# Eight more rows of the second batch's first stage in the prologue, and reads and writes on other queues: a fused spectral filter and feed-forward kernel

## The chip, the cores and the metric

The kernel runs on one core of one Trainium2 chip. The metric is the device time of one execution in microseconds; lower is better. A core has a matrix engine (PE, with its weight loads shown apart as PEld), a vector engine (DVE), an activation engine (ACT), a general engine (POOL) and a sequencer for transfers (SP). SP, ACT and POOL can all issue DMA transfers; those of one issuing engine are issued in the order of the program. Every engine works through its own list of instructions in order and waits on semaphores where it needs another's result.

## The reference

All arrays are float32 except the two weight matrices, which come as float64 (8-byte words) and are turned into float32 on the chip.

```python
X = np.fft.rfft(x, axis=1)                       # x: (8, 3008, 256)
Y = X * (filt_r + 1j * filt_i)[None, :, :]
y = np.fft.irfft(Y, n=3008, axis=1).astype(np.float32)
h = y.reshape(24064, 256) @ w_in                 # (256, 2048)
g = h - np.tanh(h)
out = (g @ w_out).astype(np.float32)             # (2048, 256)
```

## The kernel before

**The transforms.** The sequence of 3008 is split as 64 x 47 (`NQ`, `NR`). The *first stage* is, for each of the 47 residues r, a transform over the 64 positions; residues r and 47 - r are taken together as one "row" of 128 partitions, so a batch has 24 rows (`NH`). One row is one matmul: 128 x 128 matrix, 128 x 256 data. Results go to a scratch tensor in device memory, `ct1[b]`. The *second stage* goes across the rows, multiplies with the filter and goes back; its results are in `ct2[b]`. The *last stage* reads 4 rows of `ct2[b]` (tile `e2`) and makes `ut`, up to 512 tokens in transposed form: these are one *group*; a batch has 6 groups (`NC`), the kernel 48. `last(i, z)` does it: matmuls into two PSUM banks `pu` (even and odd), a copy of the odd one by ACT, an add and a subtract by DVE into `ut`.

**The feed-forward part.** Each group goes through four units (u = 0 to 3, a quarter of the 2048 hidden columns each; unit number U = 4i + u): the product with `w_in` (`up_plain` for U below 4, `up` behind), the nonlinearity on ACT and DVE (`shrink`), the product with `w_out` (`down_plain`, `down`). `up` and `down` use a seven-product scheme with prepared sums of weights, `up_plain` and `down_plain` the plain products. The weights lie in `wu` and `wd`, `[128, 7, 1024]` each: parts 0, 1, 3 and 6 hold the converted weights, parts 2, 4 and 5 (and 6, later) the sums, which `sums` writes from the first group on.

**The prologue** (up to the first unit) runs batch 0 through its first and second stage with everything kept on chip where possible. The second stage of batch 0 runs over seven slots of frequencies (loop over `g`, 0 to `last_g` = 6): `across` (transposes), `forth` (over the rows), `filtered`, and `back0` or, for the last slot, `back`. The ways back are put off by one slot (`ended`, `way_back`). Each writes its part of `ct2[0]`; `rest(a, n, queues)` reads slots a to a + n of it into `e2` with four transfers, one for each of four blocks, dealt over the queues given. Beside that the prologue converts the first five weight parts (`convert`, from the generator `early`; the order of its instructions among the others is the order in which the code calls it).

**Batch 1 and 2.** In the prologue `first1(x1)` does rows 0 to 7 of batch 1's first stage: `x1` is loaded by `load_x` on SP at g == 2; four PSUM banks of two rows each are copied by ACT into `two` (a half of the kept tile `xy`, then the tile `a1`) and written to `ct1[1]` with four transfers on SP. The other rows of batch 1 (c = 2 to 5, four rows each) and all of batch 2 are done by the generator `first(2, z2, also)`: each step (`next(firsts[2])`) is four matmuls, two ACT copies and one write issued by ACT, and starts the loads of the step after next on SP. In the main loop the places of these steps are set by the list `due`, in positions 20c + 5u + k (k = 0 to 4, five places in each unit): in group 0 a step may stand at any place that is due, later only at u < 3 and k == 2. `NX` is 6, `LEAD` 34.

**The tail of the prologue**, in program order: `rest` for slots 0 to 4 on SP, the last way back (its copies at L481, its writes at L483 on ACT and SP in turn), `rest` for the last two slots on SP, the start of `first` (two loads), the rest of the conversions, `first1(x1)`, the start of the later conversions, and eight matmuls that feed nothing (`warmer`). Then `last(0, z2)`, four more such matmuls (L1374) and the first unit. The tile tags `e1` (two or four buffers), `big` (three buffers) and `xy` (two halves in turn, `buffer("xy")`) are shared: `x1` and the later conversions use buffers that others have left.

Of the kernel before, what the change touches and what calls it, by code (L numbers as in the profile page):

```python
# [117 lines left out]
def kernel(  # L118
# [144 lines left out]
    def load_x(t, b, r, n):  # L263

        nc.sync.dma_start(t[0:64, 0:n, :], dram(x.tensor, (b * SEQ + r) * DM,
                                                [[NR * DM, 64], [1, n * DM]]))
        lo = 1 if r == 0 else 0
        if lo:
            nc.sync.dma_start(t[64:128, 0, :], dram(x.tensor, b * SEQ * DM,
                                                    [[NR * DM, 64], [1, DM]]))  # L270
        nc.sync.dma_start(t[64:128, lo:n, :], dram(x.tensor, (b * SEQ + NR - r - lo) * DM,
                                                   [[NR * DM, 64], [-DM, n - lo], [1, DM]]))
        return t
# [310 lines left out]
    def last(i, z, held=False):  # L584
# [13 lines left out]
        even, odd = banks  # L598
        for k in (1, 0) if held else (1,):
# [3 lines left out]
        u4 = ut.rearrange("p h (j n) -> p h j n", n=128)  # L603
        m = sum(w == 128 for w in widths(c))
# [3 lines left out]
        if i == 0:  # L608
            uts[i] = (ut, None, w)
            yield  # L610
            return
# [420 lines left out]
    with tc.tile_pool(name="tr", bufs=2) as tr, tc.manual_schedule():  # L1032
# [16 lines left out]
        with tc.tile_pool(name="pro", bufs=1) as pro, \  # L1049
# [172 lines left out]
            def first1(x1):  # L1222

                for r in range(0, 8, 2):
                    pf = z0("pf", [128, 2, DM])
                    for k in range(2):
                        nc.tensor.matmul(pf[:, k], f0[:, r + k], x1[:, r + k],
                                         start=True, stop=True)
# [4 lines left out]
                    ACT.copy(a1, pf)  # L1233
                    nc.sync.dma_start(
                        dram(ct1[1], r * DM, [[NH * DM, 128], [1, 2 * DM]]), a1)
                    yield
# [286 lines left out]
```

## Time and profile before

| | us |
|---|---|
| median of 3 runs | 2541.87 |
| lowest, highest | 2540.63, 2543.5 |
| profiled execution | 2542.18 |
| its span in the trace | 2540.3 |

| engine | busy us | share of the span |
|---|---|---|
| PE | 2522.6 | 99% |
| DVE | 1935.6 | 76% |
| ACT | 1694.2 | 67% |
| POOL | 1532.0 | 60% |

The trace is of one execution. Its span leaves out what lies around the program; the profiled execution's own time is 1.9 us longer than its span. Names in the trace are those of the program with the numbers left out: `x1` shows as `x`, `ct1` and `ct2` as `ct`, `a1` and `a2` as `a`. L and a number is the line of the kernel. In a timeline row the columns are start, length, engine, line, operation, output and inputs, shapes, number of instructions merged, and in brackets the idle time of the engine ahead of it with what ended it. A matmul of float32 shows as two records. The ends of matmuls are modelled, so lengths of consecutive PE rows overlap by a little; times from start to start are exact.

### The profile page before, as it was taken

To read this page: it belongs to the slowest core of one execution; us is meant where nothing else is said; L and a number is where in the kernel's file an instruction comes from. 1 tells how busy PE (TensorE), PEld (TensorE's weight loads), DVE (VectorE), ACT (ScalarE), POOL (GpSimd) and SP (SyncE) were. 2 spreads that over 40 slices of the span, in tenths; PEclk is the share of its full clock that TensorE was granted. 3 is DMA by queue.
4 is the path that set the end of the run, shared out by engine and by line. 5 is a ranking of instruction groups with operands and counts; after the bars stand their busy time and mean duration, and the time that the engine had idled before them with its cause. 6 is when DMAs were issued, how large, how long until landed. Compare 5 with 4: busy or idle time off the path is not lost.

```text
span 2540.3 us, 44575 instructions
## 1 busy us (share of the span) xinstructions
PE 2522.6 (99%) x17072; PEld 2173.1 (86%) x17072; DVE 1935.6 (76%) x2270; ACT 1694.2 (67%) x2551; POOL 1532.0 (60%) x1112
## 2 busy tenths in 40 slices
PE   9999999999999999999999999999999999999998
PEld 8678889888898888988888888898889888898887
DVE  6888877988678876888669886698866888555555
ACT  4666666667666766676667666666666666666665
POOL 5255665667556765676656665666655666455552
PEclk9999999999999999999999999999999999999999
DMA  9854224422343323342334322343123322110110
GB/s 245 261 150 117 65 54 100 112 65 53 86 108 91 82 69 89 80 112 59 80 87 105 87 56 72 96 111 89 36 72 84 92 66 53 26 31 19 25 22 19
DMA packets 333664, 211.37 MB, mean 83 GB/s; under 512 B 231645, under 2 KB 305531, under 8 KB 329793
## 3 DMA queue, kind: packets, MB, share of 16 engines
q1 hardware_dynamic: 319091, 184.93, 29.8%
q0 software_dynamic: 11120, 16.16, 2.3%
q10 hardware_dynamic: 3230, 7.34, 0.9%
q8 instruction: 136, 2.23, 0.4%
q14 instruction: 87, 0.71, 0.1%
HBM read 127.81 MB, written 83.39 MB: 83 GB/s over the span
## 4 chain that ended last, share of the span: by engine, by line
PE 96%; DVE 2%; DMA 1%; issue 0%; POOL 0%; ACT 0%; ACTq 0%; SPq 0%; POOLq 0%; DVEq 0%
PE o L821 44%; PE x L648 25%; PE z L648 12%; PE y L648 6%; PE pm L415 2%; PE pu L595 2%; PE pm L351 1%; PE o L883 1%; PE pf L308 1%; DMA filt<-in_filt_r_dram 1%; DMA x<-in_x_dram 0%; DMA ct<-e 0%; PE o L719 0%; PE x L719 0%; PE z L719 0%
## 5 line engine op out<-in xcount | busy, mean ns | idle before, releaser
L821 PE MATMUL o<-t,wd 128*128 128x256 f32 (+1 forms) x3008 | 762.7, 376 | 0.0
L619 POOL TENSOR_TENSOR t<-h 128x512 f32<-128x512 f32 (+1 forms) x184 | 303.6, 1650 | 707.3 <-DVE h L771 642.2
L771 DVE TENSOR_TENSOR h<-h,y 128x1024 f32<-128x1024 f32 (+1 forms) x384 | 571.0, 1487 | 156.4 <-ACT y L767 156.4
L821 PEld LDWEIGHTS o<-t,wd 128*128 128x128 f32 x3008 | 568.8, 190 | 84.5 <-POOL o L853 15.1
L648 PE MATMUL x<-tu,wu 128*128 128x256 f32 (+1 forms) x2256 | 571.4, 376 | 0.0
L821 PE MATMUL o<-h,wd 128*128 128x256 f32 (+1 forms) x2256 | 569.9, 375 | 0.2 <-DVE h L771 0.2
L648 PEld LDWEIGHTS x<-tu,wu 128*128 128x128 f32 x2256 | 427.4, 190 | 53.8 <-issue 3.9
L821 PEld LDWEIGHTS o<-h,wd 128*128 128x128 f32 x2256 | 428.3, 190 | 50.9 <-issue 0.8
L654 ACT COPY s<-x 128x512 f32<-128x512 f32 (+1 forms) x188 | 109.3, 581 | 517.4 <-PE x L648 517.3
L764 ACT ACTIVATE y<-y 128x1024 f32<-128x1024 f32 (+1 forms) x384 | 399.5, 1040 | 12.1
L767 ACT ACTIVATE y<-y 128x1024 f32<-128x1024 f32 (+1 forms) x384 | 399.8, 1041 | 4.6
L761 ACT ACTIVATE y<-h 128x1024 f32<-128x1024 f32 (+1 forms) x384 | 400.6, 1043 | 2.5 <-DVE h L697 1.7
L622 POOL TENSOR_TENSOR t<-h,t 128x512 f32<-128x512 f32 (+1 forms) x184 | 338.3, 1838 | 0.0
L620 POOL TENSOR_TENSOR t<-h,t 128x512 f32<-128x512 f32 (+1 forms) x184 | 310.5, 1688 | 14.4
L621 POOL TENSOR_TENSOR t<-h 128x512 f32<-128x512 f32 (+1 forms) x184 | 276.9, 1505 | 0.0
L654 ACT COPY u<-x 128x512 f32<-128x512 f32 (+1 forms) x376 | 214.1, 569 | 72.9 <-PE x L648 69.6
L697 DVE COPY h<-x 128x512 f32<-128x512 f32 (+1 forms) x188 | 127.6, 679 | 129.1 <-PE x L648 128.9
L689 DVE TENSOR_TENSOR h<-z,u 128x512 f32<-128x512 f32 (+1 forms) x188 | 127.2, 677 | 88.9 <-ACT u L654 88.5
L648 PE MATMUL x<-ut,wu 128*128 128x256 f32 (+1 forms) x752 | 194.0, 380 | 0.2 <-DVE h L697 0.2
L648 PE MATMUL z<-tu,wu 128*128 128x256 f32 (+1 forms) x752 | 190.2, 375 | 1.4 <-DVE h L705 1.4
L648 PE MATMUL y<-ut,wu 128*128 128x256 f32 (+1 forms) x752 | 190.1, 375 | 0.0
L648 PE MATMUL z<-ut,wu 128*128 128x256 f32 (+1 forms) x752 | 190.0, 375 | 0.0
(215 smaller groups left out, 2933.5 us busy)
## 6 DMA issues: line engine op xcount, KB each, us to landing
ft<-filt SPq DMA_DIRECT2D x28, 1024.0 KB
ct<-nn SPq DMA_DIRECT2D x56, 512.0 KB
e<-ct SPq DMA_DIRECT2D x47, 512.0 KB
a<-ct SPq DMA_DIRECT2D x112, 192.0 KB
out_dram<-ot SPq DMA_DIRECT2D x1248, 16.0 KB
x_sb<-in_x_dram SPq DMA_DIRECT2D x110, 128.0 KB
ct<-a SPq DMA_DIRECT2D x60, 128.0 KB
ct<-x_sb SPq DMA_DIRECT2D x60, 128.0 KB
```

The costliest lines, as they stand in the source:

```text
L619: by.tensor_sub(t[0], b[0][1], b[0][0])
L620: by.tensor_sub(t[1], b[1][1], t[0])
L621: by.tensor_sub(t[2], b[1][1], b[0][1])
L622: by.tensor_sub(t[3], b[1][0], t[1])
L648: nc.tensor.matmul(bank[:, k], wu[:, q - 1, (2 * u + k) * 128:(2 * u + k + 1) * 128], rhs[q - 1], start=(first and k == 0), stop=True, ski ...
L654: ACT.copy(t, X)
L697: V.tensor_copy(h[:, 2, :, 0:w], X)
L761: ACT.activation(y[k], ht[k], AF.Arctan, scale=TURN)
L764: ACT.activation(y[k], y[k], AF.Tanh, scale=BEND)
L767: ACT.activation(y[k], y[k], AF.Square, scale=SCALE, accum_out=y_sums[:, 2 * U + k // 2:2 * U + k // 2 + 1])
L771: V.tensor_mul(ht[k], ht[k], y[k])
L821: nc.tensor.matmul(product(q), wd[:, q - 1, (2 * u + k) * 128: (2 * u + k + 1) * 128], rhs[q - 1][:, k], start=(u == 0 and k == 0 and q == ...
```

## The change

It has six parts:

1. `load_x` takes the queue as an argument.
2. In `last`, for group 0 only, the eviction of `pu` goes by halves: copy, add and subtract for h = 0, then for h = 1.
3. `first1` takes the first row, and writes two tiles of four rows each (one transfer each, on POOL) instead of four of two rows on SP. It is called twice: for rows 0 to 7 as before, and for rows 8 to 15. Those come from a second tile, `x1b`, loaded on POOL at g == 1 (`x1` gets its buffer there too), and their results go through parts 4 and 5 of `wu`.
4. The first `rest` is issued on POOL; the second on SP and ACT in turn, and stands behind the first call of `first1`.
5. `first` no longer does rows 8 to 15 of batch 1 (c = 2 and 3), so the main loop has two steps less, and `due` has eight places in the same stretch instead of ten.
6. `warmer(8)` becomes `warmer(2)`, and the four matmuls behind `last(0, z2)` become two.

```diff
-    def load_x(t, b, r, n):
+    def load_x(t, b, r, n, queue=nc.sync):
...
@@ last @@
+        u4 = ut.rearrange("p h (j n) -> p h j n", n=128)
+        m = sum(w == 128 for w in widths(c))
+        if i == 0:
+            t = tr.tile([128, 2, CH, 64], F32, tag="e1", bufs=2, name="odd")
+            for h in range(2):
+                ACT.copy(t[:, h], odd[:, h])
+                V.tensor_add(u4[:, h, :, 0:64], even[:, h], t[:, h])
+                V.tensor_sub(u4[:, h, 0:m, 127:63:-1], even[:, h, 0:m], t[:, h, 0:m])
+            uts[i] = (ut, None, n // 2)
+            yield
+            return
...
@@ prologue @@
-            def first1(x1):
+            def first1(x1, at, tiles):
 
-                for r in range(0, 8, 2):
+                for r in range(at, at + 8, 2):
                     pf = z0("pf", [128, 2, DM])
                     for k in range(2):
-                        nc.tensor.matmul(pf[:, k], f0[:, r + k], x1[:, r + k],
+                        nc.tensor.matmul(pf[:, k], f0[:, r + k], x1[:, r + k - at],
                                          start=True, stop=True)
                     if r % 4 == 0:
-                        two = (tr.tile([128, 2, 2, DM], F32, tag="a1", bufs=1, name="a1") if r else
-                               buffer("xy").rearrange("p (m n) c -> p m n c", m=2))
-                    a1 = two[:, r // 2 % 2]
-                    ACT.copy(a1, pf)
-                    nc.sync.dma_start(
-                        dram(ct1[1], r * DM, [[NH * DM, 128], [1, 2 * DM]]), a1)
-                    yield
+                        two = tiles.pop(0)()
+                    ACT.copy(two[:, r // 2 % 2], pf)
+                    if r % 4:
+                        G.dma_start(dram(ct1[1], (r - 2) * DM, [[NH * DM, 128], [1, 4 * DM]]),
+                                    two.rearrange("p m n c -> p (m n c)"))
...
                 if g == 2:
-                    x1 = load_x(big([128, 8, DM], F32, "x1"), 1, 0, 8)
+                    load_x(x1, 1, 0, 8)
+                if g == 1:
+                    x1 = big([128, 8, DM], F32, "x1")
+                    x1b = load_x(big([128, 8, DM], F32, "x1b"), 1, 8, 8, G)
...
-            rest(0, SG * (last_g - 1), [nc.sync])
+            rest(0, SG * (last_g - 1), [G])
             way_back()
-            rest(SG * (last_g - 1), NA - SG * (last_g - 1), [nc.sync])
-            fs = first(2, z2, [(1, c) for c in range(2, NX)])
+            convert(100)
+            first1(x1, 0, [lambda: buffer("xy").rearrange("p (m n) c -> p m n c", m=2),
+                           lambda: tr.tile([128, 2, 2, DM], F32, tag="a1", bufs=1, name="a1")])
+            rest(SG * (last_g - 1), NA - SG * (last_g - 1), [nc.sync, ACT])
+            fs = first(2, z2, [(1, c) for c in range(4, NX)])
             next(fs)
-            convert(100)
-            for _ in first1(x1):
-                pass
+            first1(x1b, 8, [(lambda q=q: wu[:, q].rearrange("p (m n c) -> p m n c", m=2, n=2))
+                               for q in (4, 5)])
             late = weights(tiles1, jobs[5:], G, ahead, 4,
                            after={6: (0,), 8: (1,), 10: (2, 4)})
             next(late)
-            warmer(8)
+            warmer(2)
...
-            for _ in range(4):
+            for _ in range(2):
                 nc.tensor.matmul(warm[0:KM], mats[:, 3 * KM:4 * KM], mats[:, 3 * KM:3 * KM + 256],
                                  start=True, stop=True)
...
-            due = [4 + (LEAD - 4) * k / (NX + 4) for k in range(NX + 4)]
+            due = [4 + (LEAD - 4) * k / (NX + 2) for k in range(NX + 2)]
```

More of the change, by code (lines that the diff above doesn't have):

```diff
@@ L261, in weights @@
                 yield from sums(u)
-    def load_x(t, b, r, n):
-        nc.sync.dma_start(t[0:64, 0:n, :], dram(x.tensor, (b * SEQ + r) * DM,
-                                                [[NR * DM, 64], [1, n * DM]]))
+    def load_x(t, b, r, n, queue=nc.sync):
+        queue.dma_start(t[0:64, 0:n, :], dram(x.tensor, (b * SEQ + r) * DM,
+                                              [[NR * DM, 64], [1, n * DM]]))
         lo = 1 if r == 0 else 0
         if lo:
[L269 to L272, printed above, removed]
+            queue.dma_start(t[64:128, 0, :], dram(x.tensor, b * SEQ * DM,
+                                                  [[NR * DM, 64], [1, DM]]))
+        queue.dma_start(t[64:128, lo:n, :], dram(x.tensor, (b * SEQ + NR - r - lo) * DM,
+                                                 [[NR * DM, 64], [-DM, n - lo], [1, DM]]))
         return t
@@ L602, in last @@
             even, odd = (even, t) if k else (t, odd)
-        u4 = ut.rearrange("p h (j n) -> p h j n", n=128)
-        m = sum(w == 128 for w in widths(c))
         V.tensor_add(u4[:, :, :, 0:64], even, odd)
```

4 lines of the change are left out of this document (removed).

## The prediction

> **What bounds the kernel now.** I read the page's busy times first, then the windows stage by stage, then the engines' timelines and the waits where a window has a gap.
>
> ```profile
> span 2540.3 us, 44575 instructions
> PE 2522.6 (99%) x17072; PEld 2173.1 (86%) x17072; DVE 1935.6 (76%) x2270; ACT 1694.2 (67%) x2551; POOL 1532.0 (60%) x1112
> ```
>
> PE is busy 99% of the span, so in most stages a matmul taken away is its full time won. The change touches only the prologue (until about 80 us) and the first two token groups (80 to about 190 us), so those are read in windows. Columns: stretch, its length, then busy time and instructions of PE, PEld, DVE, ACT, POOL, then granted clock, DMA share, GB/s.
>
> ```profile
> 34.00:38.00 4.00, 4.00 (x24) 3.49 (x23) 3.86 (x7) 2.08 (x4) 0.00 (x0) 1.00 0.99 256
> 38.00:42.00 4.00, 2.87 (x13) 2.13 (x13) 3.90 (x7) 0.66 (x2) 2.38 (x3) 1.00 0.35 86
> 80.00:98.00 18.00, 18.00 (x58) 10.77 (x58) 15.45 (x31) 12.91 (x23) 2.89 (x4) 1.00 0.97 301
> 98.00:120.00 22.00, 22.00 (x68) 12.48 (x66) 20.98 (x41) 16.61 (x28) 8.18 (x13) 1.00 0.97 303
> 120.00:143.00 23.00, 22.84 (x143) 15.62 (x143) 22.20 (x45) 13.11 (x22) 10.47 (x12) 1.00 0.79 225
> 143.00:165.00 22.00, 22.00 (x118) 16.03 (x117) 17.52 (x29) 16.20 (x24) 9.21 (x9) 1.00 0.76 185
> ```
>
> From 80 to 143 us PE has no gap, but DVE is close behind it: 20.98 of 22 and 22.20 of 23 us, because the weight conversions (L183 to L201) and Strassen sums (L229, L232) run there. From 143 us DVE has room again (17.52 of 22). Two engines are near their limit in the very stretch from which the change takes PE work; on this the forecast turns.
>
> The seam between prologue and main loop is the other place. First PE, then ACT and SP (SPq rows are its DMA issues), then two pieces of the chain of waits:
>
> ```profile
> 66.55 3.62 PE L1227 MATMUL pf<-x,f 128*128 128x256 f32 x16
> 70.00 3.62 PE L1081 MATMUL warm<-f 128*128 128x256 f32 x16
> 76.05 0.33 PE L595 MATMUL pu<-gt,e 64*64 64x64 f32 x4 [2.42 <-DMA e<-ct]
> 76.71 1.15 PE L595 MATMUL pu<-gt,e 64*64 64x64 f32 x60 [0.34 <-issue]
> 77.79 1.99 PE L1374 MATMUL pt<-mats_sb 120*120 120x256 f32 x8
> 79.77 1.77 PE L719 MATMUL x<-ut,wu 128*128 128x448 f32 x4
> ```
>
> ```profile
> 68.43 0.37 ACT L481 COPY e<-pe 112x256 f32<-112x256 f32 x1 [0.94 <-PE pf L1227]
> 70.74 1.09 ACT L1233 COPY a<-pf 128x512 f32<-128x512 f32 x2
> 77.94 0.59 ACT L601 COPY odd<-pu 128x512 f32<-128x512 f32 x1 [6.11 <-PE pu L595]
> 82.96 0.67 ACT L181 ACTIVATE xy<-ft 128x512 f32<-128x512 f32 x1 [3.86 <-DMA ct<-xy]
> 66.57 0.29 SPq L1129 DMA_DIRECT2D e<-ct  x1
> 69.65 0.82 SPq L483 DMA_DIRECT2D ct<-e  x2
> 73.28 1.36 SPq L1129 DMA_DIRECT2D e<-ct  x4
> ...
> 69.65 3.61 DMA ct<-e
> 73.68 2.23 DMA e<-ct
> ```
>
> PE waits 2.42 us (and 0.34 more) for `e2`, whose last rows take this road: copies of the last way back (the second from 68.43), SP's writes of them at 69.65 and 70.10, landed 3.61 us after the first, then four reads issued one after the other on SP from 73.28 to 74.64, the last landing 2.23 us on. SP's write was late by a wait for the earlier reads on its own queue:
>
> ```profile
> SPq L483 <- DMA e<-ct: 1.3, 1, 1.3
> ```
>
> **The change part by part.** *Reads and writes on other queues.* With the first four `rest` reads on POOL, SP no longer stands behind them: its two writes go when their copies are done, the second at 68.43 + 0.37 = 68.8 instead of 70.1. Landed 3.6 us on, 72.4. The four last reads are split over SP and ACT, two each at 0.34 us, so the last is issued at 72.4 + 0.34 = 72.75 and lands 2.23 us later: 75.0, where before it was 74.3 + 2.23 = 76.5 (PE went on 0.2 us after that, at 76.71). ACT now stands at these reads until 72.4. Behind them on ACT are the four new evictions of `first1(x1b)`, at 1.09/2 = 0.55 us each: 73.1 + 2.2 = 75.3. `pu` follows both, with the 0.2 us: **75.5**, 1.2 us earlier. `convert(100)` moves ahead of other calls, but on ACT and DVE it stays between the way back and the row evictions, so their order is the old one.
>
> *The four reads moved to POOL* are free to go at 66.57 as before. POOL runs nothing then; an issue costs 0.75 us by its own rows, so the last leaves at 69.6. What a POOL transfer needs to land:
>
> ```profile
> 51.60 1.51 POOL L1145 DMA_DIRECT2D ct<-e  x2
> ct<-e POOLq DMA_DIRECT2D x6, 240.0 KB, 5.1
> less<-neg POOLq DMA_DIRECT2D x1, 24.0 KB, 5.0
> x<-in_x_dram POOLq DMA_DIRECT2D x5, 256.0 KB, 10.6
> ```
>
> Reads of 100 KB lie between the 24 KB and the 240 KB row: 5.1 us, 74.7, under 75.5 by 0.8. The row with 10.6 is from the full DMA rings of the first 15 us and is kept for a rival. The Trainium skill, page "DMA: Bandwidth & Descriptors", section "Anatomy of one DMA — SWDGE (gpsimd) path", fits 2.0 us plus bytes/436e3 to such a transfer: 2.2 us, an estimate by which the reads land at 71.8; the rows above are more than twice that, and by either the sum stays as it is.
>
> *More PE work in the gap, fewer warm-up matmuls.* First rows (16 records, 66.55 to 70.00: 3.45 us), as much for the new rows, two warm-ups at 0.43: PE is through at 74.3, before 75.5, so the added work costs nothing; its cover is what is left of the wait (1.2 us). After `pu`, two warm-ups (0.86) instead of four (1.73) lie beside the eviction of `pu`.
>
> *The split eviction.* Before, `pu` ended at 77.86 and the first product started at 79.77, 1.9 us later. Now the first product needs one half: ACT copy of 256 columns 0.37 (the L481 row), DVE add 0.42 (row below), subtract of 192 columns about 0.35: 1.2 us. The second half is through at 0.43 + 4 halves = 2.0 us; DVE is free 0.15 us later after `pu` than before.
>
> ```profile
> 123.49 0.42 DVE L619 TENSOR_TENSOR tu<-ut 128x256 f32<-128x256 f32 x1
> 120.17 1.16 PE L595 MATMUL pu<-gt,e 64*64 64x64 f32 x64
> 78.56 0.69 DVE L605 TENSOR_TENSOR ut<-pu,odd 128x512 f32<-128x512 f32 x1 [2.58 <-DMA x_sb<-in_x_dram]
> 79.17 0.55 DVE L606 TENSOR_TENSOR ut<-pu,odd 128x384 f32<-128x384 f32 x1
> ```
>
> With 1.16 us of `pu`: end 76.7, first product 77.9, **1.9 us earlier**; DVE free at 78.7 instead of 79.7, **1.0 us earlier**.
>
> *Two steps of `first` less in the main loop.* One step is eight records, 1.73 us of PE:
>
> ```profile
> 115.50 1.73 PE pf L308 x8
> ```
>
> By the due list, six steps fell in group 0 (positions 4, 7, 10, 13, 16, 19) and one at position 22; now five fall in group 0 (from 4 in steps of 3.75) and none at 22; those at 27, 32 and 42 stay. So 3.46 us of PE leave before the unit at 141.79, and PE alone would be there 1.9 + 3.46 = 5.4 us sooner. But DVE would not:
>
> ```profile
> 139.32 0.69 DVE L689 TENSOR_TENSOR h<-z,u 128x512 f32<-128x512 f32 x1
> 141.05 0.68 DVE L697 COPY h<-x 128x512 f32<-128x512 f32 x1
> 141.79 1.13 PE L648 MATMUL x<-ut,wu 128*128 128x256 f32 x4 [0.17 <-DVE h L697]
> ...
> DVE xy L183 <- ACT xy L181: 1.1, 2, 0.6
> DVE h L771 <- ACT y L767: 1.1, 2, 0.7
> DVE ut L605 <- ACT odd L601: 0.2, 1, 0.2
> ```
>
> PE already waits 0.17 us there for DVE to clear bank x (L697, done at 141.73), and bank z (L689) is cleared 0.6 us before its next use at 140.60. From 79.7 to 143.3 DVE's idle time for others is only 1.1 + 1.1 + 0.2 = 2.4 us; the steps taken away hold no DVE instruction. So DVE comes to L697 earlier by its 1.0 us of head start plus what it saves of the 2.4: between 1.0 and 3.4 us. I take 2.1: the 1.1 us of L183 should go, since half is ACT's 3.86 us wait for the write of `xy` (row 82.96), which SP issued late and POOL now issues from 71 us on, and half is conversions queued on ACT behind an eviction pair of a step that moves on. The waits of L771 are for ACT's chain and move with PE. After 143 us DVE has room, the step positions are as before and the shift stays. **DVE, not PE, decides: 2.1 us.**
>
> *The load of `x1b` at group 1*: two POOL issues from 39.33 - 6.76 = 32.6 on, 1.5 us, in POOL's idle time:
>
> ```profile
> 39.33 1.26 POOL L456 TENSOR_TENSOR nn<-nn,xy 120x512 f32<-120x512 f32 x1 [6.76 <-DVE xy L454]
> ```
>
> Behind them on POOL is that L456, not due until 39.33. The cost is on the DMA engines: 1.05 MB at the 256 GB/s of 34 to 38 us is 4.1 us of all of them, and 38 to 42 us offers 4 x 0.65 = 2.6. Between 0 and 4.1 us of delay to what follows; I take 0.4, since most fits and the filters queued there are due later. The results in `wu` columns 4 and 5 are read out before the first sums write there, well inside group 0; the second write (POOL, about 75 us) lands beside main-loop work. Both cost nothing unless a conversion were to wait for them, 5.1 us at most by the row above, from the first sum on.
>
> Sum: 2.1 - 0.4 = 1.7 us off. The profiled execution took 2542.18 us (span 2540.3), 0.3 above the median of 2541.87, so the median comes to 2541.87 - 1.7 = **2540.2 us**.
>
> **The rivals.**
> *A. PE alone decides.* If DVE does not hold PE at 140 us, because it gains all its idle time and PE's banks free sooner than the in-order reading says, the full 5.4 - 0.4 = 5.0 us come out: 2536.9 us. For it: PE waits for DVE only 0.17 us now. Against: 95% busy DVE over 45 us with nothing taken off it.
> *B. The POOL reads come last (slower).* If the four reads moved to POOL need the 10.6 us of the early loads, `e2` is complete at 69.6 + 10.6 = 80.2, not 75.5: 4.7 us later, 1.7 - 4.7 = -3.0, 2544.9 us. It turns from gain to loss from a landing of 77.2 on (7.6 us). For it: the results' writes follow on the same queue and x loads on SP at that time. Against: the DMA engines are half idle there, and 5.0 and 5.1 us in busier stretches. PE would stand idle 5.9 us in this case. The Trainium skill, page "TensorE: Matmul & The Clock Gate", section "What's actually happening", has the clock halve after an idle window of about 3.4 us and stay so for as long of busy time; by that rule, an estimate, 1.7 us more would be lost here. The trace has no gap that long: after its 2.42 us the granted clock is 1.00 (the window from 80 us).
> *C. The seam is not shortened.* If the new evictions on ACT, or the writes beside the reads, hold `pu` at 76.7, the head start of 1.2 us is gone: 0.5 us off, 2541.4 us. For it: ACT stands at a DMA wait with four evictions behind it.
> *D. The extra load delays the prologue* by its whole 4.1 us instead of 0.4: 2.0 us slower, 2543.9 us. Against: the 0.35 share at 38 to 42.
>
> **How the numbers follow.** Forecast 52%, A 25%, B 9%, C 8%, D 6%. The range 2536.4 to 2543.7 takes in A with a little more (up to 5.4 off), C, and most of D; it leaves out B and the tails beyond. No change that this kernel's measurement can tell is within 0.2%, 5.1 us. A stands on that bound: with the load's 0.4 us it is 5.0 off, without it 5.4; 15 of A's 25% are given to the latter. Faster by more: 15%. Slower by more needs B or D with still later transfers: 8%. Within: 77%.
>
> **What would show it.** Right: SP's L483 issues near 67.6 and 68.8; last `e<-ct` landing and `pu` near 75.5; first product near 77.9; eight L308 steps instead of ten; a PE wait of 2 to 3 us on DVE L689 or L697 in the unit before 140 us. Wrong: no such wait and the second group about 5 us earlier (A); `pu` released by a POOL `e<-ct` after 77 us (B); `pu` released by ACT's copies (C); the way back of the last group starting after 66.5 us (D).

## The result, and the profile after

| | before | after |
|---|---|---|
| median, us | 2542.85 (18 runs) | 2548.44 (18 runs) |
| lowest, highest | 2540.63, 2546.57 | 2543.1, 2553.69 |
| profiled execution (span) | 2542.18 (2540.3) | 2550.05 (2548.2) |

The ratio after to before is 1.002, with an interval of 1.0014 to 1.0026: the change makes the kernel slower, by some 5.6 us in the medians. The forecast was 2540.2, and the time lies above the range's end of 2543.7. In the two profiled executions the difference is 7.9 us, and the rows below say where it came in. In the changed kernel L1144, L1146, L1149 and L1150 are what L1139, L1141, L1144 and L1145 were, L1127 is L1122, L1134 is L1129, L1232 to L1238 are `first1`, and the units' lines are five higher. First the page's line of busy times for the changed kernel (us, share of the span, number of instructions):

```profile
PE 2524.7 (99%) x17056; PEld 2173.6 (85%) x17056; DVE 1934.7 (76%) x2272; ACT 1694.1 (66%) x2552; POOL 1536.2 (60%) x1122
```

PE has 16 records less and yet 2.1 us more of busy time than before: some of its matmuls took longer. The windows show where. Columns as in the prediction: stretch, length, busy time of the five engines, granted clock, DMA share, GB/s.

```profile
38.00:42.00 4.00, 2.88 (x14) 2.14 (x13) 3.90 (x7) 1.40 (x3) 1.26 (x1) 1.00 1.07 194
54.00:58.00 4.00, 4.00 (x20) 3.40 (x19) 0.31 (x1) 1.76 (x3) 1.44 (x2) 1.00 1.05 329
62.00:66.00 4.00, 2.91 (x6) 1.86 (x7) 2.67 (x4) 0.95 (x2) 2.64 (x3) 0.54 0.65 138
66.00:70.00 4.00, 4.00 (x13) 3.08 (x12) 3.86 (x7) 0.59 (x1) 0.00 (x0) 0.60 0.87 305
120.00:143.00 23.00, 23.00 (x139) 14.68 (x138) 22.35 (x46) 16.90 (x26) 16.46 (x21) 1.00 0.97 256
```

The transfer engines, free for 65% of 38 to 42 us before, are now full there; from 54 to 58 us DVE stands still (0.31 of 4 us, before 3.54); and from 62 to 70 us the granted clock is 0.54 and 0.60, where before it was 1.00. The same stretch in SP's issues, of the kernel before and then of the changed one:

```profile
42.97 2.46 SPq L1122 DMA_DIRECT2D filt<-in_filt_r_dram  x3
...
48.25 2.32 SPq L1122 DMA_DIRECT2D filt<-in_filt_r_dram  x3
```

```profile
48.97 3.08 SPq L1127 DMA_DIRECT2D filt<-in_filt_r_dram  x3
...
54.66 3.47 SPq L1127 DMA_DIRECT2D filt<-in_filt_r_dram  x3
```

SP issues the filters of the two last whole slots 6.0 and 6.4 us later. The load that did it, in the view of the tile `x1b`, with DVE's waits from 26 to 66 us behind it (us in all, times, longest):

```profile
L265 POOL DMA_DIRECT2D x1b<-in_x_dram x1: 546/546/546, 33.9 to 33.9; - x1
...
DMA to landing us min/median/max: 11.2/11.9/12.7
```

```profile
DVE nn L447 <- DMA filt<-in_filt_r_dram: 6.5, 2, 5.3
DVE xy L452 <- DMA filt<-in_filt_i_dram: 1.8, 1, 1.8
```

The load was issued at 33.9 us (forecast: from 32.6 on), and its two transfers took 11.2 and 12.7 us. DVE then waits 8.3 us for filters; before, its only wait for a transfer in this stretch was 1.5 us. The chain of waits of the changed kernel shows what that sets, to the end of the seam (start, length, what):

```profile
53.76 6.89 DMA filt<-in_filt_i_dram
...
65.42 0.85 PE pe L1144 x2
...
69.50 0.43 PE pe L1146 x2
...
75.72 4.12 DMA ct<-e
...
80.34 5.32 DMA e<-ct
```

A filter that lands at 60.65 us releases DVE (L452, from 60.73 us), then POOL and PE (PE's row at 64.21, below), whose matmuls take 0.85 us a pair until 68.6 us and 0.43 from 69.3 us on. PE's timeline gives the gaps, the last way back (L478) and the first product (L724):

```profile
62.29 1.12 PE L1144 MATMUL pe<-nn,mats_sb 120*120 120x256 f32 x2 [2.50 <-DVE nn L453]
64.21 1.21 PE L1146 MATMUL pe<-nn,mats_sb 120*120 120x256 f32 x2 [0.80 <-POOL nn L456]
...
73.22 1.04 PE L478 MATMUL pe<-xy,mats_sb 112*112 112x128 f32 x8
...
85.94 1.74 PE L595 MATMUL pu<-gt,e 64*64 64x64 f32 x60 [2.05 <-DMA e<-ct]
87.61 2.06 PE L1382 MATMUL pt<-mats_sb 120*120 120x256 f32 x4
89.46 1.77 PE L724 MATMUL x<-ut,wu 128*128 128x448 f32 x4
...
147.79 1.13 PE L653 MATMUL z<-ut,wu 128*128 128x256 f32 x4 [0.79 <-DVE h L694]
149.52 1.13 PE L653 MATMUL x<-ut,wu 128*128 128x256 f32 x4 [0.60 <-DVE h L702]
197.46 1.13 PE L653 MATMUL z<-tu,wu 128*128 128x256 f32 x4 [1.09 <-DVE h L710]
```

The last of these rows stood, before, at

```profile
189.77 1.13 PE L648 MATMUL z<-tu,wu 128*128 128x256 f32 x4 [1.12 <-DVE h L705]
```

so that four stretches can be set beside the forecast, all in us (the forecast's seam is 77.9 - 65.67 = 12.2; its 2.1 in all, less 1.9 at the seam, leaves 0.2 for the main loop):

| stretch | before | forecast | after | difference |
|---|---|---|---|---|
| start to last way back (L478) | 65.67 | +0.4 | 73.22 | +7.55 |
| last way back to first product | 14.10 | -1.9 | 16.24 | +2.14 |
| first product to the row at 189.77 | 110.00 | -0.2 | 108.00 | -2.00 |
| from there to the end of the span | 2350.5 | 0 | 2350.7 | +0.2 |
| sum | | -1.7 | | +7.9 |

How much of the 7.55 us is the clock's? From 64.21 to 69.33 us PE does six pairs in 5.12 us, which at 0.43 each, and 0.53 for the first behind a wait (its time in the third experiment), take 2.7: 2.4 us more than at full speed. But L478 also needs DVE's last subtract, which starts at

```profile
71.29 0.42 DVE L458 TENSOR_TENSOR xy<-nn 112x256 f32<-112x256 f32 x1
```

and where L478 waits for that subtract, in the experiments below, it starts 0.57 us behind its start. So L478 could not have started before 71.86, and at most 1.4 of the 7.55 us are the clock's. The other 6.2 or so are the late filters and what was late ahead of them: PE and SP were some 0.7 us late before the load was issued (one filter issue of SP goes at 31.12 us instead of 30.38).

### The profile page after: what moved, and what is told of

Same layout as the page of the kernel before. It is cut to its first block, busy times and chain, and to the rows that moved or that the text cites. A ratio compares the mean times of both kernels' runs of the same rounds, so it can differ in the third digit from the quotient of the medians.

```text
span 2548.2 us, 44545 instructions
## 1 busy us (share of the span) xinstructions
PE 2524.7 (99%) x17056; PEld 2173.6 (85%) x17056; DVE 1934.7 (76%) x2272; ACT 1694.1 (66%) x2552; POOL 1536.2 (60%) x1122
## 3 DMA queue, kind: packets, MB, share of 16 engines
q8 instruction: 136, 2.23, 0.4%
## 4 chain that ended last, share of the span: by engine, by line
PE 94%; DMA 2%; DVE 2%; issue 0%; POOL 0%; ACT 0%; ACTq 0%; SPq 0%; POOLq 0%; DVEq 0%
PE o L826 44%; PE x L653 25%; PE z L653 12%; PE y L653 6%; PE pm L415 2%; PE pu L595 2%; DMA filt<-in_filt_r_dram 1%; PE pm L351 1%; DMA x<-in_x_dram 1%; DVE h L776 0%; PE pf L308 0%; DMA filt<-in_filt_i_dram 0%; PE o L888 0%; DMA e<-ct 0%; PE pe L1146 0%
## 5 line engine op out<-in xcount | busy, mean ns | idle before, releaser
L702 DVE COPY h<-x 128x512 f32<-128x512 f32 (+1 forms) x188 | 127.6, 679 | 129.0 <-PE x L653 128.8
L694 DVE TENSOR_TENSOR h<-z,u 128x512 f32<-128x512 f32 (+1 forms) x188 | 127.2, 677 | 88.0 <-ACT u L659 87.6
```

Of the source, the lines that this page charges most:

```text
L702: V.tensor_copy(h[:, 2, :, 0:w], X)
```

## The experiments

The theory formed from these rows: the load of `x1b` pushes the filters back (the greater part), PE's wait for them brings the slow clock, and in the seam the writes of `first1`, now issued by POOL at 78.07 to 83.04 us, run beside the last reads of `e2` (DMA share 0.82 and 0.96 in the windows from 78 to 86 us) so that these take 5.3 us instead of 2.2. Rivals: the load is innocent and the moved queues are at fault; it is the queue the load is on and not its bytes; the lost time lies in the main loop. Each experiment has a run of the kernel before on the same chip beside it; "against before" is the difference of the two medians.

**1. The change without the load.** The second call of `first1` takes the rows of `x1`.

```diff
-                    x1b = load_x(big([128, 8, DM], F32, "x1b"), 1, 8, 8, G)
...
-            first1(x1b, 8, [(lambda ...) for q in (4, 5)])
+            first1(x1, 8, [(lambda ...) for q in (4, 5)])
```

> The changed kernel without the load of x1b: the second call of first1 reads x1 a second time, so rows 8 to 15 of batch 1 come out wrong and 1 MB less is read. Theory (the 1 MB on POOL makes SP's filter loads late, DVE waits for them, PE idles and its clock halves): the first matmul of the last way back (L478) is again near 65.7 us instead of 73.2, DVE waits under 1 us for filters, the granted clock is 1.00 from 62 to 70 us, and the time falls by about 7.5, to 2541. Rival (the other moved transfers or the longer tail make the loss): L478 comes at 70 us or later and the time stays above 2546.

Measured 2544.7 against 2542.62, ratio 1.0007 (0.9998 to 1.0017). The last way back starts at 68.42, and the granted clock up to there is 1.00. Of the 5.6 us some 3.5 go with the load and 2.1 stay, though the interval reaches from no loss to 4.3. Neither expectation came out whole: DVE still waits 5.9 us in two waits for one kind of filter (the longer 4.8), L478 lies 2.7 us above the theory's 65.7 and the time 3.7 above its 2541, but both below the rival's marks. The trace is no clean witness. Experiments 1, 5 and 6 run the same code up to L478 and have it at 68.42, 67.37 and 66.38 us, so the prologue varies by some 2 us from one execution to the next even without this load.

**2. The kernel before with the load alone** (nobody reads it).

```diff
+                if g == 1:
+                    load_x(big([128, 8, DM], F32, "x1b"), 1, 8, 8, G)
                 if g + 2 <= last_g:
```

> The kernel before with nothing added but the load of x1b on POOL at group 1, into a buffer that nobody reads. Theory: the load alone makes the loss in the prologue: L478 at 71 to 73 us instead of 65.7, a DVE wait of about 5 us for a filter, clock near 0.55 after it, time 2548 to 2550. Rival: the load alone fits beside the others; L478 within 1 us of 65.7 and 2543.

Measured 2546.43 against 2542.62, ratio 1.0016 (1.0006 to 1.0025): 3.8 us for the load and nothing else. DVE's waits from 26 to 70 us, and the last way back:

```profile
DVE nn L447 <- DMA filt<-in_filt_r_dram: 7.0, 2, 4.3
```

```profile
69.61 1.10 PE L478 MATMUL pe<-xy,mats_sb 112*112 112x128 f32 x8 [0.67 <-DVE xy L458]
```

The same wait for the same filters, 3.94 us of delay at L478, and nothing else of the change in it: the load alone is enough to delay the way back and the kernel. The delay isn't inherited: ahead of the load SP is 0.6 us earlier than in the kernel before (the issue at 30.38 us goes at 29.76), and from 26 to 66 us it stands 9.5 us for landings. It is less than the theory's figures (L478 at 71 to 73 us, 2548 to 2550): the granted clock stays at 1.00 from 54 to 78 us, so the slow clock isn't part of the load's price here.

**3. Warm-up matmuls ahead of the put-off way back**, so that PE's gap there is shorter.

```diff
                     next(began[3])
+                    warmer(6)
                     way_back()
```

> The changed kernel with six warm-up matmuls ahead of the way back at group 5, where PE idles 2.5 us. It parts the two halves of the loss: late filters and halved clock. If the halved clock sets the end (matmuls at 0.85 instead of 0.43 us from 62.3 to 68.8), L478 comes 3.5 us earlier, 69.7, and the time falls to 2545. If DVE, late by the filters, sets it anyway (its last subtract ended at 72.05, 1.2 us ahead of L478), the clock is 1.00 but L478 moves by 1.2 us at most and the time is 2547 to 2548.

Measured 2545.01 against 2542.62, ratio 1.0011 (1.0002 to 1.0021). DVE's waits for the filters are as long (7.5 and 0.9 us), but the clock stays at 1.00 (windows) and the gaps are shorter (PE's timeline):

```profile
62.00:66.00 4.00, 3.25 (x16) 2.41 (x14) 2.45 (x3) 1.44 (x3) 0.69 (x1) 1.00 0.87 278
66.00:70.00 4.00, 3.13 (x13) 2.40 (x14) 3.83 (x9) 0.58 (x1) 0.00 (x0) 1.00 0.87 294
```

```profile
67.54 0.69 PE L1146 MATMUL pe<-nn,mats_sb 120*120 120x256 f32 x2 [0.57 <-DVE nn L456]
68.07 0.60 PE L1144 MATMUL pe<-nn,mats_sb 120*120 120x256 f32 x2
...
71.32 1.10 PE L478 MATMUL pe<-xy,mats_sb 112*112 112x128 f32 x8 [0.50 <-DVE xy L458]
```

L478 comes 1.9 us sooner than in the changed kernel, and 5.65 later than in the one before. Of the 1.9 us DVE's subtract brings 0.5, since it comes that much sooner (70.75 instead of 71.29); the other 1.4 are what the rows above allow the clock at L478. The result lies between the two expectations: the time is the one of the first (2545), L478 is nearer to what the second allows. That the warm-ups kept the clock is plain from its column in this execution; that the time falls by it (3.4 us less than the changed kernel, intervals that overlap) is likely.

**4. The load later**, at g == 5, where two weight loads stood; these go behind the loop.

```diff
-                    x1b = load_x(big([128, 8, DM], F32, "x1b"), 1, 8, 8, G)
...
-                    ahead += [begun(tiles1, job, queue=G) for job in jobs[7:9]]
+                    x1b = load_x(big([128, 8, DM], F32, "x1b"), 1, 8, 8, G)
...
+            ahead += [begun(tiles1, job, queue=G) for job in jobs[7:9]]
             rest(0, SG * (last_g - 1), [G])
```

> The changed kernel with the same 1 MB loaded at group 5 instead of group 1, in the place of two weight loads (1 MB), which go behind the loop. All results as in the changed kernel. Theory (it is the bytes beside the filter loads, not the tail or the queues): L478 near 66, time near 2541, as without the load. Rival (1 MB more is too much wherever it stands, or the weights come too late): L478 above 68, or a PE wait for weight conversions behind 80 us, time above 2545.

Measured 2548.9 against 2542.62, ratio 1.0028 (1.0018 to 1.0039). In place of the weights it is no better: the early filters come in time, the last slot's do not (DVE's waits from 26 to 76 us, then PE's timeline).

```profile
DVE nn L447 <- DMA filt_end<-filt: 9.3, 1, 9.3
```

```profile
73.11 2.02 PE L478 MATMUL pe<-xy,mats_sb 112*112 112x128 f32 x8 [7.37 <-DVE xy L458]
```

POOL issued the load at 56.11 and 56.67 us. This place is no better; it picks another filter to be late. It is one place, and others weren't tried.

**5. Writes held back.** As the first, and the four writes of `first1` go on SP behind the reads of `e2` and the first loads of `x`.

```diff
-                        G.dma_start(dram(ct1[1], ...), two...)
+                        held.append((dram(ct1[1], ...), two...))
...
+            for to, held_in in held:
+                nc.sync.dma_start(to, held_in)
             late = weights(...)
```

> As the run without the load (x1 read twice, rows 8 to 15 of batch 1 wrong), but the four writes of first1's results are issued on SP behind the reads of e2 and the first loads of x, as in the kernel before, instead of on POOL as soon as they are copied. In the run without the load the last reads of e2 needed about 5 us to land, in the kernel before 2.2. Theory (the results' writes share the DMA engines with these reads): the last read lands within 3 us of its issue, pu goes on 2 to 3 us earlier after L478, and the time falls from 2544.7 to about 2542. Rival (the loads of x behind the reads, or the four reads on POOL, are what they share with): landing still 4.5 us or more, time 2544 to 2545.

Measured 2541.52 against 2543.21, ratio 0.9992 (0.9983 to 1.0001): 1.7 us below before, which the interval doesn't tell from nothing, where the first experiment was 2.1 above. Its last write to `ct2` goes at 69.35 us, and the last reads land 4.53 us after their issue instead of 5.32:

```profile
80.50 2.06 PE L1385 MATMUL pt<-mats_sb 120*120 120x256 f32 x4
82.35 1.84 PE L724 MATMUL x<-ut,wu 128*128 128x448 f32 x4
```

From L478 (67.37) to the first product are 14.98 us, against 17.23 in the first experiment, so in one execution of each the writes in the seam cost some 2 us. The time is the theory's, the landing the rival's (4.5 us or more), so neither came out whole. It isn't back at the forecast's 12.2, and the trace shows three things in the way. The loads of `x` still run beside the reads. ACT stands behind DVE's weight conversion and its own four copies, so that it issues its two reads at 73.75 us, where SP issued its two at 71.83. And the two later warm-ups (`pt`) take 0.93 us each: the clock is low here too.

**6. Due times as before** for the eight steps, on the first experiment's kernel.

```diff
-            due = [4 + (LEAD - 4) * k / (NX + 2) for k in range(NX + 2)]
+            due = [4 + (LEAD - 4) * k / (NX + 4) for k in range(NX + 2)]
```

> As the run without the load, with the eight steps of first left at the first eight of the old ten due times (4, 7, 10, ... 25), so that the two that are missing are missing behind 150 us, where DVE has room, and not ahead of it. Theory (up to 143 us DVE sets the pace, so PE work taken away there is partly lost in a wait for L694 and L702): these waits, 1.8 us in the run without the load, fall under 0.5 us, and from the first product to the group 2 matmuls (pu near 213 us) it takes 3.5 us less than before instead of 2; time 1.5 us lower, 2543. Rival (PE work is worth the same anywhere): waits and time unchanged.

Measured 2543.18 against 2543.21, ratio 1.0001 (0.9992 to 1.001). The time is the theory's, but its mechanism is not there. PE's waits for DVE did not go (1.7 us at L694 and L702, where under 0.5 was expected); with a new one at L710 they are 3.2 us in sum:

```profile
PE z L653 <- DVE h L710: 1.5, 1, 1.5
PE z L653 <- DVE h L694: 1.1, 2, 0.9
PE x L653 <- DVE h L702: 0.6, 1, 0.6
```

From the first product to the row behind L710 are 110.7 us, more than the first experiment's 109.05 and before's 110.0. So the lower time than in the first experiment isn't due to these positions; its product came at 81.79 us instead of 85.65, in a prologue that is the same code. What the positions are worth in time stays open.

**7. The load on SP**, behind that of `x1` at g == 2, on the changed kernel.

```diff
-                    x1b = load_x(big([128, 8, DM], F32, "x1b"), 1, 8, 8, G)
+                    x1b = big([128, 8, DM], F32, "x1b")
...
                     load_x(x1, 1, 0, 8)
+                    load_x(x1b, 1, 8, 8)
```

> The changed kernel with x1b loaded on SP right behind x1 at group 2, instead of on POOL at group 1. All results as in the changed kernel. Theory (1 MB more on the DMA engines between 30 and 66 us is the cost, from whatever queue): DVE waits several us for filters, L478 at 70 us or later, time 2546 to 2549. Rival (POOL's transfers push SP's aside, and on SP's own queue they would not): DVE's waits for filters under 1 us, L478 near 66 to 68, time near 2543.

Measured 2546.97 against 2543.21, ratio 1.0017 (1.0008 to 1.0026): still 3.8 us, DVE's waits again 7.0 and 0.9 us, and L478 at 69.56. It is not the queue: neither another queue nor an issue at 42.2 us instead of 33.9 makes a difference. That the price grows with the bytes is not shown by this. The Trainium skill, page "DMA: Bandwidth & Descriptors", section "Issuing engines are not separate DMA queues", says that transfers of all issuing engines end on the same 16 engines and interleave; these numbers agree.

**8. The kernel before with the queues and the split eviction alone**: no rows moved, nothing loaded.

```diff
-            rest(0, SG * (last_g - 1), [nc.sync])
+            rest(0, SG * (last_g - 1), [G])
...
-            rest(SG * (last_g - 1), NA - SG * (last_g - 1), [nc.sync])
+            rest(SG * (last_g - 1), NA - SG * (last_g - 1), [nc.sync, ACT])
...
-            for _ in range(4):
+            for _ in range(2):
```

(with the split of `last` as in the change)

> The kernel before with only the moved reads (the first rest on POOL, the second on SP and ACT) and the split eviction with two warm-ups instead of four; no rows moved, no load, writes of first1 on SP as before. It measures the seam by itself. As predicted: SP's L483 no longer waits, last e2 rows 1.2 us earlier, first product 12.2 us after L478 instead of 14.1, time 1 to 2 us lower than before (2541). Rival (the POOL reads land last): first product 14 us or more after L478, time not lower.

Measured 2541.51 against 2543.21, ratio 0.9993 (0.9984 to 1.0003). The queues are innocent, and by the medians worth 1.7 us, which the interval doesn't tell from nothing. From L478 (66.44) to the product (80.38) are 13.94 us, only 0.16 less than before in this one execution:

```profile
75.93 0.33 PE L595 MATMUL pu<-gt,e 64*64 64x64 f32 x4 [1.48 <-ACT a L1238]
77.28 1.31 PE L595 MATMUL pu<-gt,e 64*64 64x64 f32 x60 [1.01 <-DMA e<-ct]
78.52 2.06 PE L1379 MATMUL pt<-mats_sb 120*120 120x256 f32 x4
80.38 2.24 PE L724 MATMUL x<-ut,wu 128*128 128x448 f32 x4
```

The last of the four reads is issued at 72.90 us, earlier as the forecast had it, but it lands only at 77.14, 4.25 us later instead of 2.23. Writes of `first1` explain little of this: SP issues the first of them at 75.69 us, 1.5 us before the landing. Loads of `x` might explain it; they are issued at 72.44 to 74.40 us, beside the reads, where before they were issued behind them (from 75.09). That is argued from the order and not shown. Then the work on PE itself is slow: the clock is 0.57 from 78 to 82 us. That led to the tenth.

**9. The load of the second experiment twice.**

```diff
+                    x1b = big([128, 8, DM], F32, "x1b")
+                    load_x(x1b, 1, 8, 8, G)
+                    load_x(x1b, 1, 8, 8, G)
```

> The kernel before with the load of x1b issued twice into the same tile (2.1 MB instead of 1.05 MB; nobody reads it). Theory (bytes on full transfer engines push the filters back, 3.8 us for one load): about 2 x 3.8 = 7.6 us slower than before, 2550 us, the last way back (L478) near 73.5 instead of 65.67 and 69.6, with waits of DVE for the filters of 10 us or more in sum. Rival (the first load uses up the free share of 34 to 42 us and merely unsettles the order of the queues, so the price is a step and not by the byte): within 2 us of the single load, 2545 to 2548.

Measured 2553.4 against 2542.71, ratio 1.004 (1.0027 to 1.0054): 10.7 us, more than the 7.6 of the theory and far more than the rival's step. But it is no test of the two: the second load writes the same tile, so POOL stood at it until the first had landed, and PE behind POOL, while DVE's waits for filters were only 3.7 us. Two of the waits from 26 to 95 us:

```profile
POOL x1b L265 <- DMA x1b<-in_x_dram: 9.7, 1, 9.7
...
PE pe L1141 <- POOL nn L456: 8.0, 1, 8.0
```

So this run shows neither that the price goes by the byte nor that more bytes by themselves cost more.

**10. As the eighth, with four more warm-up matmuls** ahead of the first group.

```diff
-            warmer(8)
+            warmer(12)
```

> The queues and the split eviction alone (no rows moved), with twelve warm-up matmuls instead of eight ahead of the first group. Theory (in the seam PE's idle time, 1.5 and 1.0 us, is followed by a clock of about 0.57 in which the last of pu, the two later warm-ups and the first product take 1.4 us more): the granted clock of 78 to 82 us is 0.9 or more, first product within 1.4 us of the end of pu, and 0.5 to 1.5 us faster than with eight: 2540 to 2541. Rival (the clock falls for another reason, or the warm-ups come in the way of pu): the clock stays near 0.6 and the time is within 0.5 us of the one with eight or above it.

Measured 2542.03 against 2542.71, ratio 0.9994 (0.9985 to 1.0003). The clock from 78 to 82 us is 1.00:

```profile
76.97 1.15 PE L595 MATMUL pu<-gt,e 64*64 64x64 f32 x60 [0.92 <-DMA e<-ct]
78.05 1.12 PE L1379 MATMUL pt<-mats_sb 120*120 120x256 f32 x4
79.35 1.77 PE L724 MATMUL x<-ut,wu 128*128 128x448 f32 x4 [0.18 <-DVE ut L606]
```

From the first `pt` to the product are 1.30 us, and now it is DVE's subtract that the product waits for, as the forecast had it with 1.2 (PE's waits ahead of it are shorter too, 0.47 and 0.92 us instead of 1.48 and 1.01); in the eighth and in the changed kernel they were 1.86 and 1.85, set by PE's own slow warm-ups. The mechanism is shown in one execution of each; in the medians the two differ by less than either interval, so its worth in time isn't.

**11. The whole change with both remedies:** load kept, the writes held as in the fifth, `warmer(6)` as in the third, `warmer(6)` instead of `warmer(2)` ahead of the first group.

```diff
+                    warmer(6)
                     way_back()
...
-            warmer(2)
+            for to, held_in in held:
+                nc.sync.dma_start(to, held_in)
+            warmer(6)
```

> The change with all rows and the load kept, first1's writes on SP behind the reads of e2, six warm-up matmuls ahead of the put-off way back at g == 5 and six instead of two ahead of the first group. Theory (the losses add: about 3.2 us the slow clock after the wait for the filters, 3.2 us the writes among the reads of e2): 2548.4 - 3.2 - 3.2 = 2542, no slower than before by more than 1 us. Rival (the two overlap, since a later prologue also moves the writes): 2544 to 2545, as with the first warm-ups alone.

Measured 2546.06 against 2542.71, ratio 1.0012 (1.0003 to 1.0021). The theory's 2542 is missed by 4 us. L478 is at 72.34 (waits for the filters of 6.6 and 2.4 us, clock 1.00), the product at 85.65; the seam is 13.3 us and PE doesn't wait in it. The filters are as late as ever, and nothing here makes up for that. In this execution there is one more loss, in the main loop, where PE's two waits for DVE are followed by matmuls at 1.97 us instead of 1.13:

```profile
144.35 1.13 PE L653 MATMUL z<-ut,wu 128*128 128x256 f32 x4 [1.16 <-DVE h L694]
146.08 1.97 PE L653 MATMUL x<-ut,wu 128*128 128x256 f32 x4 [0.60 <-DVE h L702]
```

**12. Four rows instead of eight**, with held writes and `warmer(8)` ahead of the first group.

```diff
-                    x1b = load_x(big([128, 8, DM], F32, "x1b"), 1, 8, 8, G)
+                    x1b = load_x(big([128, 8, DM], F32, "x1b"), 1, 8, 4, G)
...
-            fs = first(2, z2, [(1, c) for c in range(4, NX)])
+            fs = first(2, z2, [(1, c) for c in range(3, NX)])
...
-            due = [4 + (LEAD - 4) * k / (NX + 2) for k in range(NX + 2)]
+            due = [4 + (LEAD - 4) * k / (NX + 3) for k in range(NX + 3)]
```

> The change with four rows instead of eight (rows 8 to 11: half the load, one step less in the main loop instead of two, nine due times), first1's writes on SP behind the reads of e2, eight warm-up matmuls ahead of the first group. Theory (price and gain both by the byte and the row): the load costs 1.9 us, the step gives 1.0 us, the seam 1 to 1.5 us: 2542 to 2543, the last way back near 67.5 to 69. Rival (the free share at 34 to 42 us takes 0.5 MB for nothing): the last way back near 66 to 67 and 2540 to 2541.

Measured 2545.35 against 2542.71, ratio 1.0008 (0.9999 to 1.0017), 2.4 us above the theory. Half the load isn't free: DVE waits 6.1 us for filters, and the clock falls to 0.60 from 66 to 70 us behind it. L478 comes at 70.77 us, no sooner than with the whole load in the second experiment (69.61), and SP's two filters go 3.4 and 3.7 us later than before, there 3.8 and 3.7. That speaks against a price in proportion to the bytes. The length of its seam is the one that the forecast gave (the rows of L1234 and L1086 are from the chain of waits, the others from PE's timeline):

```profile
70.77 1.04 PE L478 MATMUL pe<-xy,mats_sb 112*112 112x128 f32 x8
```

```profile
71.80 5.18 PE pf L1234 x24
76.99 3.45 PE warm L1086 x16
```

```profile
80.55 1.38 PE L595 MATMUL pu<-gt,e 64*64 64x64 f32 x64
...
83.15 1.77 PE L724 MATMUL x<-ut,wu 128*128 128x448 f32 x4 [0.17 <-DVE ut L606]
```

From L478 to `pu` 9.78 us (forecast 75.5 - 65.67 = 9.83), to the product 12.38 (12.2). But the agreement up to `pu` is luck: PE's own rows and warm-ups last until 80.44 us, and `pu` starts when they are through. The forecast had PE through 1.2 us before `pu` and let the reads and ACT's copies set it. Only the last part, 1.2 us of eviction up to DVE's subtract, is as described, here 2.60 from `pu` to the product (forecast 2.4).

No version was shown to be faster than the kernel before: the best two that compute everything, the eighth and the tenth, have intervals that hold 1.

## Why the prediction was wrong, step by step

**The load of `x1b` is the step that failed**: "Between 0 and 4.1 us of delay to what follows; I take 0.4, since most fits and the filters queued there are due later." Measured it is 3.8 us for the load alone (second experiment) and 3.8 with the load on the other queue (seventh). That is near the upper bound, 1.05 MB at the 256 GB/s of the window before, though the twelfth speaks against a price in proportion to the bytes. L478 shows it over all profiled executions: without the load it starts between 65.5 and 68.4 us (before and experiments 1, 5, 6, 8, 10), with the whole load between 69.6 and 73.2 (after and 2, 3, 4, 7, 11; 76.9 with two loads, 70.8 with half of one). Two things were misjudged. The free 65% of 38 to 42 us isn't a place of its own: the load starts at 34, in a full stretch, shares the engines with SP's loads for 12 us, and these take longer to land. From 26 to 62 us SP stands 9.9 us for landings in the changed kernel, against 3.6 before, and so issues everything behind them later. And the filters were not "due later" by enough: DVE is busy 22.96 of the 24 us from 34 to 58 in the kernel before without a wait for one, which says that they come in time, not by how much. Rival D, given 6%, was the right mechanism. Its 2543.9 lay just outside the range's 2543.7, though the text says that the range takes in most of D. The changed kernel went beyond it for the next two reasons.

**The clock.** Under B the text said that the trace had no gap long enough to slow PE. In the kernel before that was so. The late filters made a gap of 2.50 us, and the clock fell to 0.54; already the first pair behind the gap took 1.12 us, where like waits in the third experiment left it at 0.66 to 0.69. At L478 that is at most 1.4 us by the rows, and gone in the third experiment. Nor does it need the load: without it the clock fell behind short gaps at the seam (0.57 in the eighth). The Trainium skill, page "TensorE: Matmul & The Clock Gate", section "What's actually happening", has the clock fall after an idle window of about 3.4 us that runs freely. No gap at this place of the changed kernel is that long, and yet the clock fell. That it did so in some executions and not in others with like gaps would fit a window that runs by itself, but this is a guess.

**The seam**: "first product 77.9, 1.9 us earlier", measured 2.1 later counted from L478. Two parts were right: SP's writes no longer wait for the first reads (both went within 0.1 us of their copies), and the split eviction takes 1.3 us from the first `pt` where the clock is full (tenth; forecast 1.2). One was wrong, the landing of the last reads, taken over from before as 2.23 us: it is 5.32 in the changed kernel, 4.53 with the writes held (fifth) and 4.25 in the eighth. In these two the first write of `first1` is issued 2.9 and 1.5 us before the landing, so the writes are not the whole cause; loads of `x` beside the reads may be another, and no run parts them. And ACT's reads stand behind a conversion and four copies of ACT (fifth). Two things were left out. One is `first1`'s four writes, 0.5 MB each where before there were four of 0.25 MB, moved to POOL and so into the time of the last reads, which the prediction costed at nothing for the second half ("lands beside main-loop work") and mentioned under C for the rest. The other is the clock: fewer warm-ups, two and two instead of eight and four, were counted as PE time saved, when part of what they do is to keep it up: `pu` took 1.74 us instead of 1.15 and two matmuls 2.06 instead of 1.12 (tenth).

**The main loop** went as argued in kind: "DVE, not PE, decides". Eight steps instead of ten ran (64 records of L308 instead of 80 up to 202 us), DVE was busy 22.35 of the 23 us from 120 to 143, and PE waits for it at the two named places, 0.79 us at L694 (before: L689) and 0.60 at L702 (L697), 1.4 in sum where 2 to 3 were forecast. The third wait, 1.09 us at L710, was there before too (1.12 at L705). Of the 3.46 us of matmuls 2.0 came out from the first product on, where the forecast left 0.2 for this stretch. The working behind the 0.2 did not come true either. From DVE's first conversion (L183, at 79.63 us before and 89.37 after) to PE's row behind L697 or L702 it takes 62.16 us before and 60.15 after: 2.0 shorter, where the forecast had 1.1, though the wait of L183 that was to give the 1.1 is gone as it said. And DVE was free 0.1 us ahead of the late product, where the forecast had it 0.8 behind the early one (78.7 against 77.9).

**The rivals.** A is out (the waits are there), B too: the last to land were reads of ACT, not the four on POOL, whose median was 3.9 us in the stretch from 60 to 90 us. C happened in part: writes ran beside the reads, but the reads were slow with the writes held too.

## What stays open

Why the clock falls after some gaps of 1 to 2.5 us and not after others was not settled; nor was the price by the byte, since the ninth experiment also held POOL and the twelfth speaks against proportion; a step isn't excluded. Why the last reads take 4.25 us in the eighth is argued and not shown. The eleventh shows that remedies behind the load don't add up to the forecast, but in one execution, with a loss in the main loop that the third doesn't have.

## What to carry to other kernels

A load put ahead of its use costs what stands behind it: before calling it hidden, look at the slack of the transfers queued in the same stretch (when they land against when they are first waited for), not at the free share of one window. Warm-up matmuls and short waits of PE belong in the sum with the clock that follows them. Where a write is moved to another queue, ask what it now runs beside; the transfer engines are the same.

## What the runs showed of the hardware

A gap of PE of 2.50 us was followed by a first pair of matmuls of 1.12 us, and with 0.80 us more of gap 1.9 us later by a granted clock of 0.54 to 0.60 and pairs at 0.85 us instead of 0.43, for some 6.5 us in all; a gap of 2.42 us in the kernel before by none. In the eleventh experiment 1.16 and 0.60 us were enough for a spell of slow matmuls, in the changed kernel 0.79 and 0.60 at the same place were not. With four more warm-up matmuls, behind which PE waited 0.47 and 0.92 us instead of 1.48 and 1.01, the clock was 1.00 from 78 to 82 us instead of 0.57 (tenth and eighth, one execution each). And 1 MB brought in while the transfer engines were full took 11 to 13 us to land and delayed later loads on another queue by 3.7 to 6.4 us (changed kernel, second, third and eleventh experiment); half of it delayed them by 3.4 and 3.7. On either queue the kernel lost 3.8 us by it.
